# First loads moved from ScalarE's queue to SyncE's, planner durations reset, weight steps paced closer

## The chip, the cores and the metric

The kernel runs on one core of one Trainium2 chip. The metric is device microseconds of one execution, as the median of several runs. The engines are named as the profile names them: PE is TensorE (PEld its weight loads), DVE is VectorE, ACT is ScalarE, POOL is GpSimd, SP is SyncE. SPq and ACTq are the places where SP and ACT issue transfers.

## The reference

Clustered attention, followed by a softplus feed-forward layer. B, H, S, D = 4, 8, 768, 64, with 16 centroids for each head. A query sees only the keys that have the same nearest centroid.

```
q_assign = argmax(q_n @ c_n.T);  k_assign = argmax(k_n @ c_n.T)     # rows scaled to length 1
scores = where(q_assign == k_assign, (q @ k.T) / sqrt(D), -1e9)
attn = softmax(scores);  x = (attn @ v), heads put side by side     # 3072 x 512
h = x @ w_in                                                        # 512 x 2048
g = maximum(h, 0) + log1p(exp(-abs(h)))
out = g @ w_out                                                     # 2048 x 512
```

The two weights are float64 in memory; all else is float32.

## The kernel before

**Tiles.** The work is a list of 192 score tiles of 128 queries by 768 keys. A batch has two passes of three 128-row query blocks; each pass goes through 8 heads, so a pass is 24 tiles and tiles 0 to 23 are the first pass of the first batch. A tile is four score matmuls (`s`, L652), the row maximum on DVE (`negm`, L668) and the exponential on ACT (`p`, L676). The `negm` rows are a good clock: the n-th one is tile n.

**Two ways to go on.** In tiles 0 to 23 (`whole(t)`) the float32 probabilities are turned on PE (`pT`, L692), copied to SBUF by ACT or DVE (`ptf`, L248) and multiplied with raw values (L751, 12 records a tile). From tile 24 on they are split into two float16 halves by ACT (`phl`, L712) and POOL (L256). Two tiles together are transposed by one DMA on SP (`pt<-phl`, L275), and PE multiplies them with the values, 18 matmuls a tile (L755 to L757).

**Feed-forward.** When a pass has its 24 tiles, 16 steps of `h` follow (L833 to L835, 12 matmuls each), softplus on DVE and ACT, a split on ACT and POOL (`gh`), and the second product (L899 to L901) into `o`. They are spread between the tiles of later passes.

**Weights.** 32 steps turn float64 words into two float16 halves: a load of 512 KB by ACT (L270), an absolute value on ACT (L372), three integer operations on DVE (L374, L378, L384), a cast on ACT (L390) or DVE, and a subtraction on POOL (L256). Steps 0 to 15 make `wi`, 16 to 31 make `wo`. A step may not start ahead of tile `step * WPACE`.

**What sets the order.** Nothing runs as it comes: a planner (`Order`) simulates the five engines while the program is written. It takes each operation's assumed duration, given where the operation is yielded (`op("DVE", 680, ...)`), and a priority in tiles, and appends instructions to the engines' lists. The hardware then runs each list in order. So another number in the planner changes no instruction, but can change the order on every engine. `AHEAD` and `LAG` are the tiles by which feed-forward and the value products stand behind. Where the planner sees a gap over 600 ns on PE, `warm` fills part of it with matmuls whose result nobody reads (L227).

**Loads of the first batch** (`rawk`, `rawq`, `rawv`; 10 transfers of 384 KB) are issued by ACT like all loads. ACT also runs the two activations of the centroids' lengths (`cnrm`, L293 and L294).

Of the kernel before, what the change touches and what calls it, by code (L numbers as in the profile page):

```python
# [20 lines left out]
WGATE = 0  # L21
WPACE = 1.4
WDUE = 4
LAG = 4
AHEAD = 10
FIRST = 3
# [4 lines left out]
SLACK = 0  # L31
BIAS = 2000
WBIAS = 2000
# [7 lines left out]
class Order:  # L41
# [97 lines left out]
def tile_cluster_attention__then__softplus_ffn(  # L139
# [15 lines left out]
    P = 128  # L155
# [75 lines left out]
    def op(eng, ns, emit, **opt):  # L231
        return ("op", eng, ns, emit, opt)
# [10 lines left out]
    def evict(dst, src, size):  # L243

        return op(
            ("ACT", "DVE"),
            (180 + size * 0.8, 160 + size * 1.04),
            (lambda: nc.scalar.copy(dst, src), lambda: nc.vector.tensor_copy(dst, src)),  # L248
        )
# [18 lines left out]

    def load(dst, src, nbytes):
        return op("ACT", 60, lambda: nc.scalar.dma_start(dst, src), load=nbytes / 290.0)  # L270

# [9 lines left out]
    def prep_centroids():  # L281
# [4 lines left out]

        def dve(f, ns=100):
            return op("DVE", ns, f)

        yield op("DVE", 150, lambda: V.tensor_tensor(sq, cf, cf, ALU.mult))  # L290
        yield dve(lambda: V.tensor_reduce(ss, sq, AX.X, ALU.add))
# [25 lines left out]

        yield op("PE", 200, emit)
        yield op("ACT", 500, lambda: nc.scalar.copy(cents.rearrange("p a h c -> p a (h c)"), ps))
        od.set(hk)  # L320
# [15 lines left out]
    def prep_weights(step: int):  # L336
# [37 lines left out]
        yield op("DVE", 420, lambda: nc.vector.tensor_scalar(mab, mab, 3, None, ALU.logical_shift_left), shared=True)  # L374
        yield op(
            "DVE",
            680,
            lambda: nc.vector.scalar_tensor_tensor(high, high, -0x80000000, mab, ALU.bitwise_and, ALU.bitwise_or),  # L378
# [3 lines left out]
            "DVE",  # L382
            680,
            lambda: nc.vector.scalar_tensor_tensor(high, low, 29, high, ALU.logical_shift_right, ALU.bitwise_or),  # L384
# [35 lines left out]
    def prep_v(n: int):  # L420

        vk = yield from ring("vb", NP)
        rk, vf = yield from raw_tile("v", n, [P, 2, NT, D])
        yield load(vf, rows(v, n, 0, NT, 2), P * 2 * NT * D * 4)
        vb = VB[n // 2 % NP]
        raw_v[n] = vf, rk
        od.set(("vf", n))
        if n < H:
            od.cur["prio"] = H * QT
        yield op("ACT", 830, lambda: nc.scalar.copy(vb[:, :, :, D : 2 * D], vf))  # L430
        yield sub(vb[:, :, :, :D], vf, vb[:, :, :, D : 2 * D], NT * P)
# [7 lines left out]
    def turn(dst, src, name: str, on_chip: bool):  # L439

        if not on_chip:
            yield flip(dst, src.rearrange("p c d -> p (c d)"), dst.shape[1])
            return
        step = dst.shape[1] // 2
        for g in range(0, dst.shape[1], step):
            hk, ps = yield from bank(EARLY, [P, step, P], F16, f"{name}_{g}")

            def emit(g=g, ps=ps):
                for c in range(step):
                    nc.tensor.transpose(out=ps[:, c], in_=src[:, g + c], identity=eye)  # L450

            yield op("PE", 350, emit)
            yield evict(dst[:, g : g + step], ps, step * (P if dst.dtype == F32 else 100))
            od.set(hk)

    def nearest(sim, xs, heads, low: int, sfx: str):

        nt = len(xs)
        shp = [P, nt, NCL]
# [17 lines left out]
    def prep_k(n: int):  # L477

        kkey[n // 2] = yield from ring("kt", NP)
        rk, kf = yield from raw_tile("k", n, [P, 2, NT, D])  # L480
        yield load(kf, rows(k, n, 0, NT, 2), P * 2 * NT * D * 4)
        kf = kf.rearrange("p h c d -> p (h c) d")
# [37 lines left out]
    def clusters(n, ps, mask, hk):  # L520

        h = n % H
        cnt = ps[:, 2 * NT :]
        yield op("PE", 100, lambda: nc.tensor.matmul(cnt, ones, mask, start=True, stop=True))
        if h % 4 == 0:
            alive[n] = p2.tile([P, 4, NCL], F16, tag="al", name=f"al_{n}", bufs=4)
        al = alive[n - h % 4][:, h % 4 : h % 4 + 2]
        top = ps[:, :2]
        yield op(
            "DVE", 345, lambda: nc.vector.tensor_reduce(top, cnt.rearrange("p (u c) l -> p u l c", u=2), AX.X, ALU.max)  # L530
        )
        yield op("DVE", 190, lambda: nc.vector.tensor_scalar(al, top, -MASK * P, None, ALU.is_gt))
        od.set(hk)
        od.set(("al", n))

    def load_q(n: int, pi: int):

        _, c0, nt = passes[pi]
        rk, qf = yield from raw_tile("q", f"{n}_{pi}", [P, 4, nt, D])
        yield load(qf, rows(q, n, c0, nt, 4), P * 4 * nt * D * 4)  # L540
        return rk, qf
# [25 lines left out]
    def prep_q(n: int, pi: int, nh: int, qf, qt, rk):  # L567
        sfx = f"{n}_{pi}"
        nt = passes[pi][2]
        nx = nh * nt  # L570
        part = nx / 12
        qf = qf.rearrange("p h c d -> p (h c) d")
        k1 = yield from ring("n1", 2)
        n1 = p2.tile([P, nx, P], F16, tag="n1", name=f"qn1_{sfx}")
        yield op("ACT", 100 + 750 * part, lambda: nc.scalar.activation(n1[:, :, :D], qf, AF.Copy, scale=SCALE))
        yield op(
            "DVE",
            100 + 850 * part,
            lambda: nc.vector.scalar_tensor_tensor(n1[:, :, D:], qf, SCALE, n1[:, :, :D], ALU.mult, ALU.subtract),
# [12 lines left out]
        sim, best = yield from nearest(ps, [qt0[:, c] for c in range(nx)], heads, 1, f"q{sfx}")  # L592
        yield op("DVE", 345, lambda: nc.vector.tensor_tensor(sim, sim, best, ALU.is_equal))
        k2, n2 = yield from next_n2()
        n2 = n2[:, :nx]
        yield op("DVE", 345, lambda: nc.vector.tensor_scalar(n2[:, :, D : D + NCL], sim, MASK, None, ALU.mult))

        simh = sim.rearrange("p (u c) l -> p u c l", u=nh)
        if pi == 0:
# [9 lines left out]
        aq = p2.tile([P, nx, 1], F16, tag="aq", name=f"aq_{sfx}")  # L609
        yield op("DVE", 345, lambda: nc.vector.tensor_reduce(aq, sim, AX.X, ALU.max))  # L610
        od.set(hk)
        yield op(
            "POOL",
            100 + 1540 * part,
            lambda: nc.gpsimd.tensor_tensor(n2[:, :, :D], n1[:, :, :D], aq.to_broadcast([P, nx, D]), ALU.mult),
# [20 lines left out]
    def scores(t: int):  # L636
# [39 lines left out]
        yield op("ACT", 1095 if whole(t) else 900, lambda: nc.scalar.activation(p32, st[:, :, :SH], AF.Exp, bias=negm, **tot))  # L676
        od.set(sk)
        if whole(t):
# [8 lines left out]
            for j in range(2):  # L687
# [44 lines left out]
    def attend(t: int):  # L732
# [25 lines left out]

        yield op("PE", 1340 if whole(t) else 530, emit)
        od.set(("at", t))  # L760
# [15 lines left out]
        while c < 2 * nt:  # L776
            e = next((e for e in range(c, 2 * nt) if kinds[e] != kinds[c]), 2 * nt)
            weights = sums[n // 2][:, c:e] if kinds[c] else avt[:, c:e, D:]
            dst = rs[:, c:e]
            yield op("DVE", 150, lambda: nc.vector.tensor_scalar(dst, weights, 1e-9, None, ALU.add))  # L780
            c = e
# [213 lines left out]
```

## Time and profile before

| what | value |
|---|---|
| runs | 905.17 us median of 3 (903.13 to 906.0) |
| span of the profiled execution | 899.7 us, mean granted PE clock 0.994 |
| its own time beside the span | not listed; the median lies 5.5 us above the span |
| PE busy | 853.6 us, 95% |
| ACT, DVE, POOL busy | 66%, 61%, 59% |
| chain that ended last | 62% PE, 4% transposes `pt<-phl` |

A busy share is a mean over stages that have different limits. The stage rows below cut the span at tile 0, tile 24 and tile 72 and are read one by one. Windows of one line count the records that start there.

### The profile page before, as it was taken

To read this page: it belongs to the slowest core of one execution; us is meant where nothing else is said; L and a number is where in the kernel's file an instruction comes from. 1 tells how busy PE (TensorE), PEld (TensorE's weight loads), DVE (VectorE), ACT (ScalarE), POOL (GpSimd) and SP (SyncE) were. 2 spreads that over 40 slices of the span, in tenths; PEclk is the share of its full clock that TensorE was granted. 3 is DMA by queue.
4 is the path that set the end of the run, shared out by engine and by line. 5 is a ranking of instruction groups with operands and counts; after the bars stand their busy time and mean duration, and the time that the engine had idled before them with its cause. 6 is when DMAs were issued, how large, how long until landed. Compare 5 with 4: busy or idle time off the path is not lost.

```text
span 899.7 us, 21002 instructions
## 1 busy us (share of the span) xinstructions
PE 853.6 (95%) x8701; PEld 557.6 (62%) x8701; DVE 547.2 (61%) x1044; ACT 595.2 (66%) x920; POOL 528.9 (59%) x359
## 2 busy tenths in 40 slices
PE   6999977899888999999999999999999999999997
PEld 6788854666666556566666665666665665655554
DVE  5999885777767455575665565657665655433331
ACT  4887876777766757777667677787767676633330
POOL 5323576688766577677667577687666675512110
PEclk9999998999999999999999999999999999999999
DMA  6335499999986599999988999999977776610000
GB/s 223 120 118 119 110 219 199 193 178 218 220 180 138 126 202 182 185 215 204 178 149 163 153 176 187 205 202 192 175 151 153 121 127 137 123 31 15 22 1 36
DMA packets 392527, 135.94 MB, mean 151 GB/s; under 512 B 368880, under 2 KB 385264, under 8 KB 392432
## 3 DMA queue, kind: packets, MB, share of 16 engines
q1 hardware_dynamic: 370672, 98.95, 62.3%
q10 hardware_dynamic: 21760, 35.66, 13.2%
q8 instruction: 68, 1.11, 0.5%
q14 instruction: 27, 0.22, 0.1%
HBM read 35.68 MB, written 6.29 MB: 47 GB/s over the span
## 4 chain that ended last, share of the span: by engine, by line
PE 62%; DMA 4%; DVE 1%; issue 1%; POOL 1%; ACT 1%; POOLq 0%; ACTq 0%
PE s L652 8%; PE o L899 8%; PE o L901 8%; PE o L900 8%; PE h L833 7%; PE h L834 7%; PE h L835 7%; DMA pt<-phl 4%; PE mbank L755 3%; PE mbank L757 3%; PE mbank L756 2%; POOL phl L256 1%; DVE ot L919 0%; PE sim_q L464 0%; PE sim_q L463 0%
## 5 line engine op out<-in xcount | busy, mean ns | idle before, releaser
L256 POOL TENSOR_TENSOR phl<-p,phl 128x768 f16<-128x768 f32 x168 | 278.4, 1670 | 100.5 <-ACT phl L712 81.7
L668 DVE TENSOR_REDUCE negm<-s 128x1 f32<-128x768 f32 x192 | 182.9, 954 | 61.6 <-PE s L652 58.3
L676 ACT ACTIVATE p<-s,negm 128x768 f32<-128x768 f32 x192 | 172.5, 900 | 64.7 <-DVE negm L668 49.8
L256 POOL TENSOR_TENSOR gh<-fg,gh 128x768 f16<-128x768 f32 x64 | 107.1, 1675 | 144.7 <-ACT gh L876 144.6
L833 PE MATMUL h<-xT,wi 128*128 128x384 f16 x512 | 167.5, 327 | 5.5 <-DVE fg L865 5.5
L835 PE MATMUL h<-xT,wi 128*128 128x384 f16 x512 | 167.6, 327 | 0.0
L834 PE MATMUL h<-xT,wi 128*128 128x384 f16 x512 | 167.6, 327 | 0.0
L652 PE MATMUL s<-kt,qt 128*128 128x384 f16 x768 | 156.0, 325 | 3.4 <-ACT p L676 3.0
L712 ACT CAST phl<-p 128x768 f16<-128x768 f32 x168 | 136.4, 829 | 33.2 <-DMA pt<-phl 30.8
L901 PE MATMUL o<-wo,gh 128*128 128x512 f16 x384 | 145.5, 379 | 1.1 <-POOL gh L256 1.1
L899 PE MATMUL o<-wo,gh 128*128 128x512 f16 x384 | 145.5, 379 | 0.6 <-DVE ot L919 0.6
L900 PE MATMUL o<-wo,gh 128*128 128x512 f16 x384 | 145.5, 379 | 0.0
L855 ACT ACTIVATE fa<-fa 128x384 f32<-128x384 f32 x128 | 66.6, 520 | 109.9 <-DVE fa L853 109.5
L853 DVE TENSOR_SCALAR fa<-h 128x384 int32<-128x384 int32 x128 | 71.1, 556 | 110.1 <-PE h L835 109.8
L755 PE MATMUL mbank<-vb,pt 128*128 128x65 f16 x1008 | 109.1, 193 | 17.5 <-DMA pt<-phl 17.5
L755 PEld LDWEIGHTS <-pt 128*128 128x128 f16 x1008 | 93.8, 98 | 32.4 <-DMA pt<-phl 21.7
L756 PE MATMUL mbank<-vb,pt 128*128 128x64 f16 x1008 | 109.0, 193 | 0.0
L757 PE MATMUL mbank<-vb,pt 128*128 128x65 f16 x1008 | 108.7, 195 | 0.0
L865 DVE SCALAR_TENSOR_TENSOR fg<-h,fa 128x384 f32<-128x384 f32 x128 | 70.6, 552 | 59.2 <-ACT fa L856 54.4
L652 PEld LDWEIGHTS <-qt 128*128 128x128 f16 x768 | 71.7, 98 | 48.0 <-issue 4.8
L756 PEld LDWEIGHTS <-pt 128*128 128x128 f16 x1008 | 93.4, 97 | 10.6 <-issue 0.2
L757 PEld LDWEIGHTS <-pt 128*128 128x128 f16 x1008 | 93.5, 97 | 0.0
(121 smaller groups left out, 1277.1 us busy)
## 6 DMA issues: line engine op xcount, KB each, us to landing
wo<-in_moe_w_in_dram ACTq DMA_DIRECT2D x16, 512.0 KB, 3.6
wo<-in_moe_w_out_dram ACTq DMA_DIRECT2D x14, 512.0 KB, 5.9
rawk<-in_k_dram ACTq DMA_DIRECT2D x16, 384.0 KB, 5.0
rawq<-in_q_dram ACTq DMA_DIRECT2D x16, 384.0 KB, 5.0
rawv<-in_v_dram ACTq DMA_DIRECT2D x16, 384.0 KB, 5.7
out_dram<-ot SPq DMA_DIRECT2D x24, 256.0 KB, 2.6
pt<-phl SPq DMA_TRANSPOSE x84, 6.7
wraw<-in_moe_w_out_dram ACTq DMA_DIRECT2D x2, 512.0 KB, 4.9
```

Of the source, the lines that this page charges most:

```text
L256: [lambda e=e: e.tensor_tensor(dst, a, b, ALU.subtract) for e in (nc.gpsimd, nc.vector)],
L652: nc.tensor.matmul(st[:, j, :SH], qt[:, s, i], kt[:, s, NT // 2 * j : NT // 2 * (j + 1)], start=(s == 0), stop=(s == 1),)
L668: yield op("DVE", 950, lambda: nc.vector.tensor_reduce(negm, st[:, :, :SH], AX.XY, ALU.max, negate=True))
L755: nc.tensor.matmul(av, pt[:, 0, c], vb[:, c, D : 2 * D + 1], start=(c == 0), stop=False)
L756: nc.tensor.matmul(av[:, :D], pt[:, 0, c], vb[:, c, :D], start=False, stop=False)
L757: nc.tensor.matmul(av, pt[:, 1, c], vb[:, c, D : 2 * D + 1], start=False, stop=(c == NT - 1))
L833: nc.tensor.matmul(hp, w[0], x[0], start=(c == 0), stop=False)
L834: nc.tensor.matmul(hp, w[0], x[1], start=False, stop=False)
L835: nc.tensor.matmul(hp, w[1], x[0], start=False, stop=(c == NP - 1))
L899: nc.tensor.matmul(po, g[0], wo[:, f, 0, 0], start=(f == f0), stop=False)
L900: nc.tensor.matmul(po, g[0], wo[:, f, 0, 1], start=False, stop=False)
L901: nc.tensor.matmul(po, g[1], wo[:, f, 0, 0], start=False, stop=(f == f0 + NF // 2 - 1))
```

## The change

The loads of batch 0 (`n < H`, or pass 0 for queries) are issued by SP; all others stay on ACT. Most assumed durations get other values, the engines no longer start at time 0 in the planner, and five constants change. No instruction's kind or size changes.

```
-WPACE = 1.4
-WDUE = 4
-LAG = 4
-AHEAD = 10
+WPACE = 0.8
+WDUE = 2
+LAG = 6
+AHEAD = 8
...
-BIAS = 2000
+BIAS = 1000
...
-        self.free = dict.fromkeys(self.LAT, 0.0)
+        self.free = {"PE": 1800.0, "DVE": 2500.0, "ACT": 2000.0, "POOL": 4800.0, "SP": 1000.0}
...
-            (180 + size * 0.8, 160 + size * 1.04),
+            (155 + size * 0.855, 155 + size * (1.04 if wide else 0.52)),
...
-    def load(dst, src, nbytes):
-        return op("ACT", 60, lambda: nc.scalar.dma_start(dst, src), load=nbytes / 290.0)
+    def load(dst, src, nbytes, first=False):
+
+        if first:
+            return op("SP", 500, lambda: nc.sync.dma_start(dst, src), load=nbytes / 340.0)
+        return op("ACT", 350, lambda: nc.scalar.dma_start(dst, src), load=nbytes / 340.0)
...
-        yield load(vf, rows(v, n, 0, NT, 2), P * 2 * NT * D * 4)
+        yield load(vf, rows(v, n, 0, NT, 2), P * 2 * NT * D * 4, n < H)
...
-            680,
+            760,
             lambda: nc.vector.scalar_tensor_tensor(high, high, -0x80000000, mab, ALU.bitwise_and, ALU.bitwise_or),
```

Line numbers shift by 4 to 6: L248 is then L249, L374 L378, L378 L382, L384 L388, L668 L674.

**ACT at the start of the program.** `rawk`, `rawq`, `rawv` are the first batch's loads, `kn` the first use of a load. Before:

```order
L270 DMA rawk_130<-in_k_dram 128x2x384
L270 DMA rawq_0_131<-in_q_dram 128x4x192
L270 DMA wo<-in_moe_w_in_dram 128x512
L270 DMA rawv_132<-in_v_dram 128x2x384
L293 ACTIVATE cnrm<-csg 128x1
L270 DMA rawk_133<-in_k_dram 128x2x384
L294 ACTIVATE cnrm<-cnrm 128x1
L270 DMA rawv_134<-in_v_dram 128x2x384
L319 COPY cents<-centsT 128x384
L496 CAST kn_0_137<-rawk_125 128x12x64
L575 ACTIVATE qn_0_0_142<-rawq_0_126 128x6x64
```

Now:

```order
L167 ACT_TABLE_LOAD
L274 DMA wo<-in_moe_w_in_dram 128x512
L297 ACTIVATE cnrm<-csg 128x1
L298 ACTIVATE cnrm<-cnrm 128x1
L501 CAST kn_0_136<-rawk_125 128x12x64
L581 ACTIVATE qn_0_0_141<-rawq_0_126 128x6x64
L581 ACTIVATE qn_2_0_142<-rawq_0_126 128x6x64
L434 CAST vb_104<-rawv_127 128x12x64
```

Ten issues left ACT's list and stand on SP behind the centroids' load, one weight load stands ahead of `cnrm`, and the first cast no longer stands behind the copy of the centroids (`cents`).

**DVE at tiles 12 to 15**, in the first pass. `wi` and `wo` rows belong to weight steps, `ptf` and `qt` rows are copies out of PSUM. Before:

```order
L668 TENSOR_REDUCE negm_0_1217<-s_0_1180 128x1
L384 SCALAR_TENSOR_TENSOR wo<-wo 128x512
L374 TENSOR_SCALAR wi<-wi 128x512
L248 COPY ptf_1_1169<-pT_2_0_1220 128x384
L668 TENSOR_REDUCE negm_1_1245<-s_1_1219 128x1
L579 SCALAR_TENSOR_TENSOR qn_0_1_1192<-rawq_1_1181,qn_0_1_1192 128x12x64
L248 COPY ptf_0_1235<-pT_0_0_1236 128x384
L248 COPY ptf_0_1235<-pT_1_0_1264 128x384
L378 SCALAR_TENSOR_TENSOR wo<-wo,wi 128x512
L668 TENSOR_REDUCE negm_2_1274<-s_2_1244 128x1
```

Now:

```order
L674 TENSOR_REDUCE negm_0_1245<-s_0_1189 128x1
L249 COPY qt_0_158<-qT_6_0_0_1296 128x384
L382 SCALAR_TENSOR_TENSOR wo<-wo,wi 128x512
L378 TENSOR_SCALAR wi<-wi 128x512
L249 COPY qt_0_158<-qT_6_0_3_1319 128x384
L388 SCALAR_TENSOR_TENSOR wo<-wo 128x512
L382 SCALAR_TENSOR_TENSOR wo<-wo,wi 128x512
L249 COPY ptf_1_1313<-pT_1_1_1342 128x384
L674 TENSOR_REDUCE negm_1_1340<-s_1_1316 128x1
L388 SCALAR_TENSOR_TENSOR wo<-wo 128x512
L378 TENSOR_SCALAR wi<-wi 128x512 x2
L382 SCALAR_TENSOR_TENSOR wo<-wo,wi 128x512
```

Between two neighbouring row maxima there now stand more weight rows.

**SP where tiles 46 to 49 are transposed**, at the start of the second batch. `pt` rows are the transposes of two tiles, `kt` and `qt` those of keys and queries, `xT` those of attention's result. Before:

```order
L275 DMA_TRANSPOSE pt_5_3317<-phl_4_3165 128x24x128
L275 DMA_TRANSPOSE kt_2764<-n_1_114 128x12x128
L275 DMA_TRANSPOSE pt_1_3414<-phl_0_3207 128x24x128
L275 DMA_TRANSPOSE kt_3227<-kn_14_3226 128x12x128
L275 DMA_TRANSPOSE pt_0_3512<-phl_2_3333 128x24x128
```

Now:

```order
L279 DMA_TRANSPOSE pt_5_3322<-phl_4_3066 128x24x128
L279 DMA_TRANSPOSE qt_2_2825<-n_0_112 128x12x128
L279 DMA_TRANSPOSE kt_3257<-kn_12_3256 128x12x128
L279 DMA_TRANSPOSE xT_2528<-xn_1_3532 128x6x128
L279 DMA_TRANSPOSE kt_3451<-kn_14_3450 128x12x128
L279 DMA_TRANSPOSE kt_3257<-n_1_114 128x12x128
L279 DMA_TRANSPOSE pt_1_3654<-phl_0_3573 128x24x128
```

Between the pair of tiles 46 and 47 and the pair 48 and 49 there stood one other transpose; now there stand five.

More of the change, by code (lines that the diff above doesn't have):

```diff
@@ L285, in prep_centroids, with dve @@
         V = nc.vector
-        def dve(f, ns=100):
+        def dve(f, ns=195):
             return op("DVE", ns, f)
-        yield op("DVE", 150, lambda: V.tensor_tensor(sq, cf, cf, ALU.mult))
+        yield op("DVE", 1050, lambda: V.tensor_tensor(sq, cf, cf, ALU.mult))
         yield dve(lambda: V.tensor_reduce(ss, sq, AX.X, ALU.add))
@@ L316, in emit @@
                 nc.tensor.transpose(out=ps[:, a], in_=cb[:, a].rearrange("p j d -> p (j d)"), identity=eye)
-        yield op("PE", 200, emit)
-        yield op("ACT", 500, lambda: nc.scalar.copy(cents.rearrange("p a h c -> p a (h c)"), ps))
+        yield op("PE", 580, emit)
+        yield op("ACT", 480, lambda: nc.scalar.copy(cents.rearrange("p a h c -> p a (h c)"), ps))
         od.set(hk)
@@ L452, in turn @@
             yield op("PE", 350, emit)
-            yield evict(dst[:, g : g + step], ps, step * (P if dst.dtype == F32 else 100))
+            yield evict(dst[:, g : g + step], ps, step * P)
             od.set(hk)
@@ L458, in nearest @@
         nt = len(xs)
+        ns = 145 + 17.5 * nt
         shp = [P, nt, NCL]
@@ L480, in prep_k @@
         rk, kf = yield from raw_tile("k", n, [P, 2, NT, D])
-        yield load(kf, rows(k, n, 0, NT, 2), P * 2 * NT * D * 4)
+        yield load(kf, rows(k, n, 0, NT, 2), P * 2 * NT * D * 4, n < H)
         kf = kf.rearrange("p h c d -> p (h c) d")
@@ L523, in clusters @@
         cnt = ps[:, 2 * NT :]
-        yield op("PE", 100, lambda: nc.tensor.matmul(cnt, ones, mask, start=True, stop=True))
-        if h % 4 == 0:
-            alive[n] = p2.tile([P, 4, NCL], F16, tag="al", name=f"al_{n}", bufs=4)
+        yield op("PE", 180, lambda: nc.tensor.matmul(cnt, ones, mask, start=True, stop=True))
+        if n - h % 4 not in alive:
+            alive[n - h % 4] = p2.tile([P, 4, NCL], F16, tag="al", name=f"al_{n - h % 4}", bufs=4)
         al = alive[n - h % 4][:, h % 4 : h % 4 + 2]
@@ L529, in clusters @@
         yield op(
-            "DVE", 345, lambda: nc.vector.tensor_reduce(top, cnt.rearrange("p (u c) l -> p u l c", u=2), AX.X, ALU.max)
+            "DVE", 360, lambda: nc.vector.tensor_reduce(top, cnt.rearrange("p (u c) l -> p u l c", u=2), AX.X, ALU.max)
         )
@@ L539, in load_q @@
         rk, qf = yield from raw_tile("q", f"{n}_{pi}", [P, 4, nt, D])
-        yield load(qf, rows(q, n, c0, nt, 4), P * 4 * nt * D * 4)
+        yield load(qf, rows(q, n, c0, nt, 4), P * 4 * nt * D * 4, pi == 0)
         return rk, qf
@@ L609, in prep_q @@
         aq = p2.tile([P, nx, 1], F16, tag="aq", name=f"aq_{sfx}")
-        yield op("DVE", 345, lambda: nc.vector.tensor_reduce(aq, sim, AX.X, ALU.max))
+        yield op("DVE", ns, lambda: nc.vector.tensor_reduce(aq, sim, AX.X, ALU.max))
         od.set(hk)
@@ L675, in scores @@
             tot["accum_out"] = sums[n // 2][:, n % 2 * nt + i]
-        yield op("ACT", 1095 if whole(t) else 900, lambda: nc.scalar.activation(p32, st[:, :, :SH], AF.Exp, bias=negm, **tot))
+        yield op("ACT", 1105 if whole(t) else 895, lambda: nc.scalar.activation(p32, st[:, :, :SH], AF.Exp, bias=negm, **tot))
         od.set(sk)
@@ L757, in emit @@
                 nc.tensor.matmul(av, pt[:, 1, c], vb[:, c, D : 2 * D + 1], start=False, stop=(c == NT - 1))
-        yield op("PE", 1340 if whole(t) else 530, emit)
+        yield op("PE", 1310 if whole(t) else 530, emit)
         od.set(("at", t))
@@ L779, in attend @@
             dst = rs[:, c:e]
-            yield op("DVE", 150, lambda: nc.vector.tensor_scalar(dst, weights, 1e-9, None, ALU.add))
+            yield op("DVE", 220, lambda: nc.vector.tensor_scalar(dst, weights, 1e-9, None, ALU.add))
             c = e
```

34 lines of the change are left out of this document (18 added, 16 removed).

## Prediction

> **What bounds the kernel now.** I read the page's shares, then the busy time by stage, then PE's waits in the stage that loses most, then the rows at the stage's ends. The stages are cut at the row maxima of tiles 0, 24 and 72, and at 860 us.
>
> ```profile
> 29.20 0.95 DVE L668 TENSOR_REDUCE negm<-s 128x1 f32<-128x768 f32 x1
> 103.03 0.94 DVE L668 TENSOR_REDUCE negm<-s 128x1 f32<-128x768 f32 x1
> 312.35 0.96 DVE L668 TENSOR_REDUCE negm<-s 128x1 f32<-128x768 f32 x1 [0.99 <-PE s L652]
> ...
> 0.00:29.20 29.20, 20.70 (x328) 19.10 (x329) 17.81 (x83) 16.68 (x26) 18.13 (x23) 0.94 0.60 199
> 29.20:103.00 73.80, 70.73 (x717) 62.66 (x715) 68.39 (x136) 59.71 (x122) 21.34 (x20) 1.00 0.43 115
> 103.00:312.35 209.35, 182.70 (x2198) 128.63 (x2197) 147.61 (x258) 150.54 (x229) 145.80 (x98) 0.98 0.91 182
> 312.35:860.00 547.65, 545.21 (x5235) 328.56 (x5234) 305.13 (x556) 360.59 (x533) 338.75 (x218) 1.00 0.81 151
> 860.00:899.70 39.70, 34.23 (x233) 18.70 (x231) 8.29 (x14) 7.65 (x13) 4.92 (x3) 1.00 0.06 21
> ```
>
> Columns: stretch, its length, busy PE, PEld, DVE, ACT, POOL, granted clock, DMA share, GB/s. PE is idle for 8.5 us in the head, 3.1 in the first pass, 26.7 in the middle, 2.4 from tile 72 to 860 us and 5.5 in the tail. Behind tile 72 the kernel is PE and nothing else. In the first pass DVE is busy for 68.4 of 73.8 us, as much a bound as PE. In the middle the DMA engines are busy for 91%, PE for 87%.
>
> Part of PE's busy time is filler:
>
> ```profile
> 29.20:103.00 73.80, 6.33 (x96) 5.50 (x93) 1.00 0.43 115
> 103.00:312.35 209.35, 32.19 (x523) 29.42 (x523) 0.98 0.91 182
> 312.35:860.00 547.65, 0.00 (x0) 0.00 (x0) 1.00 0.81 151
> 877.29 3.52 PE L227 MATMUL mbank<-ones,eye 128*128 128x120 f16 x64
> ```
>
> These are the rows of L227 alone. A filler takes 3.52/64 = 0.055 us, so the middle's 523 take 28.8. With the 26.7 idle, PE has nothing useful to do for 55 of 209 us there. What it waits for, where the planner put no filler:
>
> ```profile
> PE mbank L755 <- DMA pt<-phl: 15.0, 7, 5.7
> PE h L833 <- DVE fg L865: 5.5, 8, 1.6
> ...
> 142.18 10.06 SPq L275 DMA_TRANSPOSE pt<-phl  x1
> 150.90 0.24 PE L755 MATMUL mbank<-vb,pt 128*128 128x65 f16 x1 [5.69 <-DMA pt<-phl]
> ```
>
> The middle is bound by transposes that share the DMA engines with loads. One took 10 us to issue, and PE stood still for 5.7 us.
>
> PE's list has the same useful matmuls before and after, and 843 fillers for 852, which is 0.5 us. So the change is worth what PE's idle time changes by, and less than 46 us.
>
> **Loads from SP, and ACT's new order at the start.** Now the first cast stands at 10.83 us:
>
> ```profile
> 0.74 0.39 SPq L186 DMA_DIRECT2D cf<-in_centroids_dram  x1
> 0.77 0.45 ACTq L270 DMA_DIRECT2D rawk<-in_k_dram  x1
> 3.85 0.15 DVE L292 TENSOR_SCALAR csg<-css 128x1 f32<-128x1 f32 x1
> 4.41 1.28 ACTq L270 DMA_DIRECT2D wo<-in_moe_w_in_dram  x1
> 6.50 0.20 ACT L293 ACTIVATE cnrm<-csg 128x1 f32<-128x1 f32 x1 [4.49 <-issue]
> 7.47 0.38 ACTq L270 DMA_DIRECT2D rawv<-in_v_dram  x1
> 10.46 0.48 ACT L319 COPY cents<-centsT 128x384 f16<-128x384 f16 x1 [3.17 <-PE centsT L316]
> 10.83 0.84 ACT L496 CAST kn<-rawk 128x768 f16<-128x768 f32 x1
> ...
> DMA to landing us min/median/max: 3.6/6.7/8.6
> ```
>
> The last row is that of `rawk` in the first 40 us. Its earliest landing is 3.6 us behind the issue, at 4.4, while the cast waits for the copy of the centroids in its queue. That hangs on `cnrm`, which waited 4.49 us behind issues. Now the cast stands behind `cnrm` alone: `csg` is there at 4.00, two activations and the gap between them take it to about 4.9, and `rawk`, issued by SP at 1.13, lands at 4.7. That is 5.9 us earlier. SP's ten issues at about 0.5 us end near 6.1, and the last load lands by 6.1 + 8.6 = 14.7, no later than now (7.47 + 8.6). Nothing is queued on SP behind them until the first transpose of the first pass, so SP pays nothing. The ends are 0 (tile 0 waits for something unmoved) and -5.9. DVE gets four more copies ahead of tile 0, and the centroids' copy now stands behind more casts, so I take **-4**.
>
> The Trainium skill (DMA: Bandwidth & Descriptors, "Issuing engines are not separate DMA queues") says that transfers from all issuing engines interleave on the same 16 DMA engines, and that a second issuing engine saves only issue time. By that the data come no earlier, and if landing were the limit this term would be 0 and the sum 4 us less good. Here the earliest landing, 4.4 us, is far ahead of its use at 10.83, so issue time and queue order are what counts.
>
> **Weight steps closer, `WPACE` and `WDUE`.** Up to tile 24 DVE's order held 15, 15 and 13 rows of L374, L378 and L384; now it holds 20 of each. Their busy time in the first pass, in this order:
>
> ```profile
> 29.20:103.00 73.80, 6.38 (x15) 1.00 0.43 115
> 29.20:103.00 73.80, 11.18 (x15) 1.00 0.43 115
> 29.20:103.00 73.80, 9.80 (x13) 1.00 0.43 115
> ```
>
> Five by 0.43, five by 0.75 and seven by 0.75 us make 11.1 us more DVE work in the first pass. Copies out of PSUM stay about even (21 and 22). ACT gains seven casts and four absolute values and loses six copies, and has 14 us idle; POOL gains seven subtractions and has 52 idle. DVE has only 5.4 us idle. If all of it were used, the pass grows by 5.7; if the busy share stays at 93%, by 12.0. Waits between engines seldom vanish when an engine gets fuller; still, some idle time should be used: **+9.5**.
>
> PE gets 167 more fillers there (order rows from tile 0 to 24: 267 for 100), 9.2 us, so the loss will look like filler.
>
> **Fewer loads in the middle.** Six of sixteen weight loads leave it for the first pass, where the DMA engines are busy for only 43%. Their price:
>
> ```profile
> q1 hardware_dynamic: 95223, 24.26, 68.3%
> q10 hardware_dynamic: 7073, 13.48, 22.4%
> ...
> wo<-in_moe_w_out_dram ACTq DMA_DIRECT2D x14, 512.0 KB, 5.9
> ```
>
> These are the middle's queues. q10, the loads, takes 22.4% of 209.35 = 46.9 us for 13.48 MB, 3.5 us per MB, so 1.82 us for 512 KB; six are 10.9 us. If the DMA engines set the stage's length, it is -10.9; if the chain of score, maximum, exponential, split and transpose does, it is 0. At 91% busy, with 15.0 us of PE waiting for `pt`, I take **-10.9**. Seven weight steps less on DVE and POOL come off engines that are 70% busy and cost nothing.
>
> **`AHEAD`, `LAG` and the durations.** Ahead of tile 72 PE's order had 360 matmuls of L833 to L835 and 108 of L899 to L901; now 330 and 168. Value products are equal. Their spacing:
>
> ```profile
> 243.08 0.33 PE L833 MATMUL h<-xT,wi 128*128 128x384 f16 x1
> 243.24 0.33 PE L834 MATMUL h<-xT,wi 128*128 128x384 f16 x1
> ...
> 872.97 0.38 PE L900 MATMUL o<-wo,gh 128*128 128x512 f16 x1
> 873.19 0.38 PE L901 MATMUL o<-wo,gh 128*128 128x512 f16 x1
> ```
>
> Thirty by 0.16 less and sixty by 0.22 more are 8.4 us of work done earlier, out of a stretch that is all PE. It is worth -8.4 if it fills waits in the middle, and 0 if it pushes tile 72 back by as much. The 55 us without useful work leave room, but its inputs need not be ready in time: **-4.5**. The tail's order is the same, at nothing.
>
> **The sum**: -4 + 9.5 - 10.9 - 4.5 - 0.5 = -10.4, so a span near 889 us, and 5.5 above it a median of **895**.
>
> One more thing lies inside the range. After the stall at 150.90, PE is slow:
>
> ```profile
> 152.17 0.53 PE L834 MATMUL h<-xT,wi 128*128 128x384 f16 x1
> 152.49 0.53 PE L835 MATMUL h<-xT,wi 128*128 128x384 f16 x1
> ...
> 156.04 0.53 PE L834 MATMUL h<-xT,wi 128*128 128x384 f16 x1
> ```
>
> Spacing is 0.32 for 0.16 us for at least 5.1 us, so the spell cost about 2.6 us beside the wait. If this stall goes, it comes off too; a new one of this length would add it.
>
> The Trainium skill (TensorE: Matmul & The Clock Gate, "What's actually happening") says that an idle window of about 3.4 us halves PE's clock, and a busy one of that length restores it. By that figure the spell costs 1.7 us. The trace has it longer, and its number stands.
>
> **Rivals.**
> - *DVE in the first pass decides; the middle gives nothing back* (slower). For it: 68.4 of 73.8 us; and 5.5 us of PE's waits in the middle are for softplus on DVE, which no load delays. Against it: the 10 us issue and the `pt` waits. Time: -2 + 12.0 + 0 + 0 - 0.5 = +9.5, 914.7. It decides once tile 24 is late by more than the middle returns: at +6 or more against less than 6.
> - *They cancel.* SP's order has five other transposes between the pairs of tiles 46/47 and 48/49, where one stood. Each moves 6 or 12 blocks, a quarter or half of a pair's 24, so four more stop the flow of tiles for about one and a half pairs. If PE's feed-forward backlog doesn't cover that, the relief of 10.9 is lost there: -10.4 + 10.9 = +0.5, 905.7.
> - *The middle's waits go as well.* If the durations now fit the chip, PE finds its inputs in time. Then the 15.0 for `pt` and the 2.6 of the slow spell go too, instead of the 10.9: -4 + 9.5 - 17.6 - 8.4 - 0.5 = -21, 884. Against it: transposes still fill 68% of the middle.
> - *The change does nothing.* The orders differ on every engine, so it isn't a separate case; it is within the second.
>
> **Chances.** 0.3% is 2.7 us, about what a measurement of this kernel tells from no change. My sum (between -3 and -15): 0.40. The larger gain: 0.22. Cancelled: 0.14. Slower: 0.24. So faster 0.62, same 0.14, slower 0.24. From the bounds, the sum's own range goes from -5.9 + 5.7 - 10.9 - 8.4 - 0.5 = -20 to 0 + 12.0 - 10.9 - 0 - 0.5 = +0.6. The range reaches into both neighbours, leaving a tenth on each side: 881 to 912. The likeliest case's own is 885 to 906.
>
> **What would show it.** Tile 0's `negm` near 25 us and the first cast near 5. Tile 24 near 108.5 with DVE over 93% busy and more filler. Tile 72 at 307 to 311, 10 weight loads between it and tile 24, under 10 us of PE waiting for `pt`, no spell of 0.32 spacing in the middle. I am wrong if tile 24 is as early as tile 0's gain says (the DVE term), if tile 72 comes behind 312 with the DMA share well under 0.9 (the DMA term), or if PE is idle for more than 5 us behind tile 72.

## The result, and the profile after

The changed kernel took 899.54 us, the median of 20 runs (894.53 to 909.69), against 904.76 for the kernel before in the same series (20 runs, 896.84 to 909.92). The ratio is 0.9941 with a 95% interval of 0.992 to 0.9963: faster by about 0.6%, where the prediction forecast 895.0 in a range from 881 to 912. Here and below, a ratio leaves out the executions that were more than 1.5% above the fastest of their kernel, while medians and ranges count all, so a ratio is not quite the quotient of two medians. The profiled execution after lasts 899.86 us and its span is 897.6, so 2.2 us lie outside the span.

The stages after, cut at the row maxima of tiles 0, 24 and 72 (27.3, 110.6 and 320.7 us) and at 860 us; columns as in the prediction's stage rows:

```profile
27.29 0.95 DVE L674 TENSOR_REDUCE negm<-s 128x1 f32<-128x768 f32 x1
...
320.66 0.96 DVE L674 TENSOR_REDUCE negm<-s 128x1 f32<-128x768 f32 x1 [0.26 <-PE s L658]
```

```profile
0.00:27.30 27.30, 21.76 (x321) 19.73 (x322) 19.27 (x85) 15.43 (x25) 18.45 (x23) 0.94 0.69 233
27.30:110.60 83.30, 77.69 (x869) 69.02 (x869) 77.88 (x157) 62.96 (x127) 29.31 (x26) 1.00 0.48 128
110.60:320.70 210.10, 186.72 (x2072) 127.45 (x2072) 143.34 (x242) 140.65 (x212) 138.39 (x92) 0.96 0.91 172
320.70:860.00 539.30, 538.71 (x5214) 326.58 (x5213) 309.96 (x560) 362.98 (x539) 334.94 (x218) 1.00 0.81 152
860.00:897.60 37.60, 32.52 (x224) 17.75 (x222) 7.20 (x13) 6.67 (x11) 4.92 (x3) 1.00 0.06 22
```

The head is 1.9 us shorter, the first pass 9.5 longer, the middle 0.75 longer, and everything behind tile 72 takes 576.9 us for 587.35, 10.4 less. PE's filler (rows of the filler line alone, by the same columns for PE and PEld) moved from the middle to the first pass:

```profile
27.30:110.60 83.30, 16.62 (x267) 15.31 (x267) 1.00 0.48 128
110.60:320.70 210.10, 22.92 (x348) 21.62 (x348) 0.96 0.91 172
```

In the middle, PE's longest waits (total us, times, longest) and the queues and weight loads:

```profile
PE mbank L761 <- DMA pt<-phl: 10.3, 3, 5.0
PE s L658 <- ACT p L682: 5.6, 7, 2.5
...
PE h L839 <- DVE fg L871: 2.8, 5, 0.7
```

```profile
q1 hardware_dynamic: 99055, 25.68, 72.6%
q10 hardware_dynamic: 5462, 10.17, 17.8%
...
wo<-in_moe_w_out_dram ACTq DMA_DIRECT2D x8, 512.0 KB, 5.2
...
wraw<-in_moe_w_out_dram ACTq DMA_DIRECT2D x2, 512.0 KB, 6.1
```

The ten weight loads that were forecast are there (8 and 2). The waits for `pt` fell from 15.0 to 10.3 us and from seven to three, but those left are long ones.

**The books.** PE's time splits into useful work, waiting, filler (0.055 us each), and time lost to the granted clock (one minus the clock, times the length, summed over windows of 2.5 us; called half clock, since the clock is at half in these spells). Half clock while PE is idle counts in both rows. In us, before and after:

| | head | first pass | middle | behind tile 72 | sum |
|---|---|---|---|---|---|
| PE idle | 8.5, 5.5 | 3.1, 5.6 | 26.7, 23.4 | 7.9, 5.7 | 46.1, 40.2 |
| filler | 8.3, 7.8 | 5.3, 14.7 | 28.8, 19.1 | 4.7, 4.7 | 47.1, 46.4 |
| half clock | 1.7, 1.7 | 0, 0 | 3.4, 8.5 | 0, 0 | 5.1, 10.2 |

What is left is 801.3 and 800.8 us: the same useful work. So the 2.1 us between the two spans are 5.9 less idle, 0.7 less filler, 5.1 more half clock, and 0.5 in the remainder. In the middle, idle and filler fell by 13.0 us, half clock took 5.1 back, and the 8.4 us of feed-forward that now run ahead of tile 72 used what was left; that is why the middle is as long as before and the stretch behind it shorter.

The two profiled executions stand only 2.1 us apart while the medians stand 5.2 apart. In the runs since, 1.8 us lie outside the span of the kernel before, so its profile (899.7) was of an execution near 901.5, one of its shorter ones. Its clock was high as well: 0.994 in the profile, and 0.990 as the mean of the 87 executions of this kernel that ran beside the experiments, on three chips; only 13 of them reach 0.994. After, the profile has 0.989 and the mean of the 20 executions is 0.987. One minus the mean clock, times the span, is 9.3 us of half clock before and 11.7 after. By this estimate usual executions stand about 2.4 us apart in half clock, where the two profiled ones stand 5.1 apart.

### The profile page after: what moved, and what is told of

The parts are those of the page before. It is cut to its first block, busy times and chain, and to the rows that moved or that the text cites. A ratio compares the mean times of both kernels' runs of the same rounds, so it can differ in the third digit from the quotient of the medians.

```text
span 897.6 us, 20963 instructions
## 1 busy us (share of the span) xinstructions
PE 857.4 (96%) x8692; PEld 560.5 (62%) x8692; DVE 557.6 (62%) x1051; ACT 588.7 (66%) x913; POOL 526.0 (59%) x359
## 4 chain that ended last, share of the span: by engine, by line
PE 70%; DVE 6%; DMA 6%; POOL 2%; issue 2%; ACT 2%; POOLq 0%; DVEq 0%; ACTq 0%
PE s L658 10%; PE o L907 9%; PE o L905 8%; PE o L906 8%; PE h L839 8%; PE h L840 8%; PE h L841 8%; DMA pt<-phl 6%; PE mbank L761 3%; PE mbank L763 3%; PE mbank L762 3%; DVE negm L674 1%; POOL phl L257 1%; DVE wo L382 1%; PE mbank L227 1%
## 5 line engine op out<-in xcount | busy, mean ns | idle before, releaser
L674 DVE TENSOR_REDUCE negm<-s 128x1 f32<-128x768 f32 x192 | 182.6, 953 | 52.0 <-PE s L658 47.1
L718 ACT CAST phl<-p 128x768 f16<-128x768 f32 x168 | 136.4, 828 | 28.8 <-DMA pt<-phl 27.3
L761 PE MATMUL mbank<-vb,pt 128*128 128x65 f16 x1008 | 110.6, 194 | 10.6 <-DMA pt<-phl 10.3
L762 PE MATMUL mbank<-vb,pt 128*128 128x64 f16 x1008 | 110.6, 193 | 0.0
L763 PE MATMUL mbank<-vb,pt 128*128 128x65 f16 x1008 | 110.3, 195 | 0.0
```

The source lines that it names most:

```text
L674: yield op("DVE", 950, lambda: nc.vector.tensor_reduce(negm, st[:, :, :SH], AX.XY, ALU.max, negate=True))
L761: nc.tensor.matmul(av, pt[:, 0, c], vb[:, c, D : 2 * D + 1], start=(c == 0), stop=False)
L762: nc.tensor.matmul(av[:, :D], pt[:, 0, c], vb[:, c, :D], start=False, stop=False)
L763: nc.tensor.matmul(av, pt[:, 1, c], vb[:, c, D : 2 * D + 1], start=False, stop=(c == NT - 1))
```

## Experiments

All ratios are to the kernel before on the same chip, with 95% intervals. No ratio to the kernel after was measured; where two ratios are set against each other, they come from different chips, and each has its interval.

**The loads alone, without a new plan.** The kernel before, with the ten first loads issued by SP. The planner still counts them as ACT's 60 ns, so its order doesn't change.

```
+        if first:
+            return op("ACT", 60, lambda: nc.sync.dma_start(dst, src), load=nbytes / 290.0)
...
-        yield load(vf, rows(v, n, 0, NT, 2), P * 2 * NT * D * 4)
+        yield load(vf, rows(v, n, 0, NT, 2), P * 2 * NT * D * 4, n < H)
```

> The kernel before with every list in its old order, but the ten first loads issued by SP. Only the queue moves, the plan does not. If the free ACT queue is worth something by itself, tile 0 comes 1 to 3 us earlier than 29.2 and the ratio is 0.996 to 0.999. Rival: the head is bound by the casts and subtractions that follow, or the middle swallows the gain: 0.999 to 1.002. What the kernel with the loads alone replanned (0.989) gains beyond this is then the planner's other order.

898.34 us (12 runs), 0.9961 [0.9922, 0.9999]. Row maxima of tiles 0, 47, 48, 60 and 72, of this kernel and then of the kernel before:

```profile
26.32 0.94 DVE L670 TENSOR_REDUCE negm<-s 128x1 f32<-128x768 f32 x1
...
194.61 0.95 DVE L670 TENSOR_REDUCE negm<-s 128x1 f32<-128x768 f32 x1
197.28 0.96 DVE L670 TENSOR_REDUCE negm<-s 128x1 f32<-128x768 f32 x1
...
263.12 1.81 DVE L670 TENSOR_REDUCE negm<-s 128x1 f32<-128x768 f32 x2
...
311.51 0.96 DVE L670 TENSOR_REDUCE negm<-s 128x1 f32<-128x768 f32 x1 [0.99 <-PE s L654]
```

```profile
201.41 0.95 DVE L668 TENSOR_REDUCE negm<-s 128x1 f32<-128x768 f32 x1
204.08 0.96 DVE L668 TENSOR_REDUCE negm<-s 128x1 f32<-128x768 f32 x1
...
264.25 0.94 DVE L668 TENSOR_REDUCE negm<-s 128x1 f32<-128x768 f32 x1
```

Tile 0 is 2.9 us earlier (26.32 against 29.20) and tile 48 still 6.8 (197.28 against 204.08); by tile 60 only 1.1 are left, by tile 72 0.8. A gain at the head is carried to the second batch, and most of it is given back there. At ACT's start in this kernel:

```profile
7.60 0.48 ACT L321 COPY cents<-centsT 128x384 f16<-128x384 f16 x1 [3.16 <-PE centsT L318]
7.98 0.83 ACT L498 CAST kn<-rawk 128x768 f16<-128x768 f32 x1
```

The copy of the centroids moved from 10.46 to 7.60, by as much as tile 0.

**The loads back on ACT, in the new plan.** The kernel after; the planner still counts them as SP's 500 ns.

```
-            return op("SP", 500, lambda: nc.sync.dma_start(dst, src), load=nbytes / 340.0)
+            return op("SP", 500, lambda: nc.scalar.dma_start(dst, src), load=nbytes / 340.0)
```

> The changed kernel with every list in the same order, but the ten first loads issued by ACT again, at the place where the planner put them. If the head's gain comes from ACT's queue freed of issues (about 0.5 us each, ten of them), tile 0 comes 2 to 5 us later than the 27.3 us of the changed kernel and the ratio to the kernel before rises from 0.994 to 0.996 to 0.999. Rival: the gain at the head is given back in the first pass, which DVE bounds, or the move of the loads was never what counted; then the ratio stays at 0.993 to 0.995.

899.84 us (12 runs), 0.9989 [0.9954, 1.0024]. The median is that of the kernel after; the ratio is 0.5% higher, and the two intervals overlap from 0.9954 to 0.9963. What the edit costs is not settled: nothing by the medians, 0.5% by the ratios. The trace:

```profile
30.26 0.95 DVE L674 TENSOR_REDUCE negm<-s 128x1 f32<-128x768 f32 x1
...
230.55 0.94 DVE L674 TENSOR_REDUCE negm<-s 128x1 f32<-128x768 f32 x1
...
284.68 0.96 DVE L674 TENSOR_REDUCE negm<-s 128x1 f32<-128x768 f32 x1 [0.99 <-PE s L658]
```

```profile
227.70 0.96 DVE L674 TENSOR_REDUCE negm<-s 128x1 f32<-128x768 f32 x1
...
284.29 0.96 DVE L674 TENSOR_REDUCE negm<-s 128x1 f32<-128x768 f32 x1 [0.99 <-PE s L658]
```

Above are tiles 0, 48 and 60 of this kernel, below tiles 48 and 60 of the kernel after. The 3.0 us at tile 0 are there as 2.9 at tile 48 and 0.4 at tile 60. Both traces give the same reading: the head's 3 us reach the second batch and are mostly lost between tiles 48 and 60.

**The loads with a new plan.** The kernel before with the loads planned and issued on SP, `op("SP", 500, ...)`, and nothing else.

> The kernel before with the first ten loads on SP alone (planned with 500 ns each on SP). If the head's 2 to 4 us reach the end, tile 0 is at 25 to 27.5 us and the ratio 0.995 to 0.998. Rival: the middle swallows them, or the planner's other order decides: 0.998 to 1.005.

896.53 us (6 runs), 0.9887 [0.9844, 0.9929]. It is the lowest ratio of a kernel that does all the work; its interval overlaps that of the kernel after, so it is shown to beat the kernel before and not the kernel after. The head has nothing to do with it: in its profiled execution tile 0 stands at 35.7 us, 6.5 later than before, and tile 72 at 327.8. That execution is the longest of the six. Its books are 40.8 idle, 48.5 filler, 8.6 half clock. Ratio and tile 0 lie outside both expected ranges.

**The pace alone, in the old plan and out of the new one.** Before with `WPACE` 0.8 and `WDUE` 2; after with 1.4 and 4.

> The kernel before with WPACE 0.8 and WDUE 2 alone. If pulling the weight steps forward is what shortens the kernel (loads leave the middle, which the DMA engines bound), the ratio is 0.988 to 0.994, with tile 24 5 to 9 us later than 103.0. Rival: what the middle gains, the longer first pass takes: 0.997 to 1.003.

906.22 us (12 runs), 1.0006 [0.9974, 1.0038]; tile 0 at 29.4 us, tile 24 at 112.0, tile 72 at 324.9. The first pass takes 82.6 us for 73.8, of which 3.4 are half clock. Alone, the pace takes only two weight loads out of the middle (14 issues between tiles 24 and 72 for 16), not six as the whole change does.

> The changed kernel with WPACE 1.4 and WDUE 4 again, planned anew: 102 fillers more (5.6 us), six or seven weight loads back in the middle. If loads in the middle cost their full DMA price, as the light loads showed (12.5 us for 12.7), tile 24 comes near 101, but tile 72 no earlier than 320, and the ratio is 0.998 to 1.006. Rival: the shorter first pass makes up for it, as in the kernel before with the new pace alone (1.0006): 0.992 to 0.997.

903.18 us (12 runs), 0.9995 [0.9968, 1.0022]; tile 0 at 27.2 us, tile 24 at 104.4, tile 72 at 322.9. The first pass takes 77.3 us for 83.3, and 16 weight loads are back in the middle. So the pace is worth nothing in the old plan, and about 0.5% in the new one (0.9995 against 0.9941, whose intervals just fail to overlap). In both plans it makes the first pass longer, by 8.8 and by 6.0 us; what comes back for that hangs on the rest of the plan.

**The durations alone.** Before with the new durations, start times and `BIAS`, the loads still on ACT (350 ns).

> The kernel before with the new assumed durations, start times and BIAS alone (loads on ACT, old pace, LAG and AHEAD). If durations that fit the chip remove waits by themselves, PE's idle time falls under 35 us from 46 and the ratio is 0.985 to 0.995. Rival: the planner's order is as good or bad as before, and 79 more fillers cost up to 4 us: 0.998 to 1.008.

914.77 us (6 runs), 1.0102 [1.0065, 1.0139]. Tile 0 stands at 39.1 us. The new durations alone made the kernel slower by 1%, more than either expected range. The parts alone (loads 0.9887 or 0.9961, pace 1.0006, durations 1.0102) do not add up to the whole: each makes its own order on every engine and its own number of fillers (882, 834 and 931, where the whole change has 843).

**`LAG` and `AHEAD` back.** After with 4 and 10.

> The changed kernel with LAG 4 and AHEAD 10 again, planned anew. If feed-forward moved ahead is what the change gains (8.4 us of work ahead of tile 72), the ratio goes back to 0.999 to 1.005. Rival: these two only push work about, and idle, filler and cold time stay within 3 us of the changed kernel's 97 us: 0.991 to 0.997.

899.61 us (12 runs), 0.9947 [0.9917, 0.9976]: no different from the kernel after. It does not test what the feed-forward ahead of tile 72 is worth: in its trace 320 matmuls of `h` and 162 of `o` stand there, 332 and 168 in the kernel after, so the new plan took back only 3.2 of the 8.4 us.

**Lighter weight loads in the middle.** After; the eight `wo` loads of the middle bring 64 of 512 columns, and most of those weights are left out.

```
+        cols = WC // 8 if step >= 22 and room < 8 else WC
+        yield load(raw64[:, :cols], src[:, c, e * WC : e * WC + cols], P * WC * 8)
```

> The changed kernel in the same order, but eight weight loads of steps 22 to 29 bring only 64 of 512 columns, so that 8 x 7/8 x 1.82 = 12.7 us of load work leave the DMA engines in the middle stage (tiles 24 to 71). It leaves out most of those weights. If the share of busy DMA engines sets the middle's length, the middle shrinks from 210 us to 197 to 201 and the ratio falls to 0.980 to 0.985. Rival: the middle is set by the chain of score, maximum, exponential, split and transpose and by where the planner put the work of the second batch, and loads only stretch what nobody waits for; then the middle shrinks by less than 4 us and the ratio is 0.989 to 0.995.

887.52 us (6 runs), 0.982 [0.9781, 0.9859]. Seven eighths of eight loads at 1.82 us are 12.7 us of transfer; the span is 12.7 us shorter than that of the kernel after, and tile 72 comes 12.5 earlier:

```profile
308.16 0.96 DVE L675 TENSOR_REDUCE negm<-s 128x1 f32<-128x768 f32 x1 [0.26 <-PE s L659]
```

By the ratios it is 1.2%, about 11 us. So in an order that is kept, a load taken out of the middle is worth its full time. The books show how: idle falls from 40.2 to 32.8 us and half clock from 10.2 to 5.1. One place in both traces, first the kernel after (a weight load on ACT's queue, three transposes on SP with the time in which the first of them landed, PE's next product with values, PE's next steps of `h`), then this kernel (the same first transpose, its landing, the transpose of keys, the product):

```profile
171.44 0.38 ACTq L274 DMA_DIRECT2D wo<-in_moe_w_out_dram  x1
```

```profile
169.82 3.87 SPq L279 DMA_TRANSPOSE pt<-phl  x1
...
175.44 7.41 SPq L279 DMA_TRANSPOSE kt<-kn  x1
183.01 4.91 SPq L279 DMA_TRANSPOSE pt<-phl  x1
...
DMA to landing us min/median/max: 13.2/13.2/13.2
```

```profile
183.03 0.23 PE L761 MATMUL mbank<-vb,pt 128*128 128x65 f16 x1 [4.98 <-DMA pt<-phl]
...
184.31 0.53 PE L840 MATMUL h<-xT,wi 128*128 128x384 f16 x1
184.62 0.53 PE L841 MATMUL h<-xT,wi 128*128 128x384 f16 x1
```

```profile
170.87 3.51 SPq L279 DMA_TRANSPOSE pt<-phl  x1
...
DMA to landing us min/median/max: 9.1/9.1/9.1
...
176.17 3.59 SPq L279 DMA_TRANSPOSE kt<-kn  x1
...
180.03 0.20 PE L762 MATMUL mbank<-vb,pt 128*128 128x65 f16 x1 [0.92 <-DMA pt<-phl]
```

PE waits here for the transpose issued at 169.82, not for one behind it. With the full loads it lands 13.2 us behind its issue, PE waits 4.98 us for it, and then works at a spacing of 0.31 for 0.16. With the light ones it lands after 9.1 us, PE waits 0.92 and keeps its clock. The transpose of keys, issued while it was on its way, takes 7.41 us to issue in the one and 3.59 in the other.

**Lighter integer operations in the first pass.** After; the three integer operations of weight steps 0 to 19 on 64 of 512 columns, which leaves most of the conversion out.

```
+        part_ = WC // 8 if step < 20 else WC
...
+        yield op("DVE", 450, lambda: nc.vector.tensor_scalar(mab[:, :part_], mab[:, :part_], 3, None, ALU.logical_shift_left), shared=True)
```

> The changed kernel in the same order, but the three integer operations on DVE of weight steps 0 to 19 work on 64 of 512 columns, which takes some 30 us of DVE work out of the first pass. It leaves out most of that conversion. If DVE sets the first pass, tile 24 comes earlier than 110.6 us until PE with its fillers is the limit (5.6 us idle there): 105 to 107, and the ratio falls to 0.987 to 0.990 if the rest keeps it. Rival: the first pass is set by PE's list with its 14.7 us of filler; then tile 24 moves by less than 2 us and the ratio stays at 0.992 to 0.995.

895.34 us (12 runs), 0.9904 [0.9872, 0.9936]. The first pass of its profiled execution, in the stage columns:

```profile
28.40:109.10 80.70, 76.88 (x864) 68.55 (x864) 55.37 (x156) 61.98 (x126) 27.34 (x26) 1.00 0.47 129
```

DVE's busy time falls from 77.88 to 55.37 us, and the pass shortens by 2.6. With DVE at 69% the pass is nearly as long as with DVE at 93%, so in this order DVE's work alone does not set its length. More than 5.6 us could not come back, though: the filler stays in PE's list, and with it PE is busy for 77.7 of the 83.3 us in the kernel after. Whether the planner would put the filler there with less DVE work is not tested.

**No filler in the first pass.** After, with none of the fillers between tiles 0 and 24.

```
+        first_pass = ("sc", 0) in od.ev and ("sc", 23) not in od.ev
+        if gap > WARM_FROM and not first_pass:
```

> The changed kernel in the same order, without the 257 fillers that stand between tile 0 and tile 24 (14.1 us at 0.055). If PE's list with its fillers sets the first pass, it shrinks from 83.3 us to 70 to 76 and the ratio to the kernel before falls to 0.982 to 0.990, if the middle keeps it. Rival: the fillers only cover waits for DVE and ACT; then the first pass shrinks by less than 3 us, PE is idle instead, and the ratio stays at 0.992 to 0.998, or is worse if PE goes to half clock there.

908.59 us (12 runs), 1.0027 [0.999, 1.0064]. Its profiled execution, 916.39 us, is the longest of the twelve, so its lengths are above the usual ones; its first pass:

```profile
28.40:123.30 94.90, 80.46 (x612) 68.32 (x612) 76.61 (x157) 62.93 (x127) 29.53 (x26) 0.82 0.38 112
```

In this execution the granted clock falls from 1.00 to 0.82 and the pass grows from 83.3 to 94.9 us. The fall is not its own alone: the mean clock of all twelve is 0.974, for 0.987 after. So leaving the filler out gains nothing, since the clock falls without it; how long the pass would be without filler at a full clock this run does not show.

**More filler.** After with `WARM_SHARE` 0.9 for 0.65 (1176 fillers for 843).

> The changed kernel in the same order, but with 1176 fillers instead of 843, in the same places: 333 by 0.055 are 18 us more filler. If they fall into time in which PE would be idle or cold, the spells at half clock get fewer and the time stays within 3 us or falls: ratio 0.989 to 0.997. Rival: the gaps that the planner sees are already filled or are not there on the chip, and each filler delays useful work: 8 to 18 us longer, ratio 1.003 to 1.014.

897.11 us (12 runs, 894.5 to 898.63), 0.9911 [0.9884, 0.9938]. Stages 29.7 to 115.5 to 316.6 us:

```profile
29.70:115.50 85.80, 81.90 (x973) 74.31 (x972) 77.53 (x156) 63.24 (x127) 28.89 (x26) 1.00 0.45 124
115.50:316.60 201.10, 187.87 (x2212) 130.97 (x2211) 139.96 (x242) 140.93 (x212) 139.56 (x92) 0.99 0.97 181
```

The first pass is 2.5 us longer and the middle 9.0 shorter, at a clock of 0.99 for 0.96. Its books: 27.2 idle, 64.7 filler, 5.4 half clock, together 97.2 where the kernel after has 96.8. Over its twelve executions the mean clock is 0.9925, so half clock is less in usual executions too. The 3.0 us between the two spans lie in the remainder (797.4 for 800.8), which the books don't explain. The ratios differ by 0.3% and their intervals overlap: no gain is shown, but the executions lie closer together.

**More filler in the loads' own plan.** `WARM_SHARE` 0.9 in the kernel that has the loads planned on SP (1230 fillers for 882).

> The kernel before with the first ten loads planned and issued on SP, and with 1230 fillers for 882 in the same places. If filler ends spells at half clock and takes only idle time, as it did for the changed kernel (0.991 for 0.994), idle and cold time fall by more than the 19 us that the filler costs, and the ratio is 0.982 to 0.988. Rival: this order has fewer cold spells to end (8.6 us in its profile), so the filler costs what it brings: 0.988 to 0.993.

903.66 us (12 runs), 1.001 [0.9976, 1.0043], above both expected ranges. The mean granted clock of its profiled execution is 0.998 against 0.991 without the added filler. Idle falls by 14.0 us to 26.8 and half clock by 6.9 to 1.7, but filler rises by 19.2 to 67.7, so nearly all is taken back. The profiled pair flatters the added filler (spans 896.1 and 899.4, the latter its kernel's longest execution): the mean clock is 0.994 over the twelve executions with it and 0.9945 over the six without, so usual executions lose no less to half clock. Then 19.2 us of filler stand against 14.0 of idle, an estimate of 5.2 us longer, where the medians stand 7.1 apart (903.66 and 896.53).

## Why the prediction came near, step by step

**The total.** 895.0 was forecast and 899.54 measured, inside the range and on the forecast side. The sum forecast -10.4 us; the medians show half of it, -5.2, and the profiled pair -2.1. The 5.5 us that the prediction laid between span and median are not time outside the span, which is 1.8 to 2.2 us; the rest is that the execution profiled before was a short one. With 2 us its span near 889 would have meant 891; the 5.5 made the forecast the median before less 10.4, so this misreading did the total good. The range also holds the times of two rivals (884 and 905.7), so the time alone does not bear out the mechanism; the terms do that, one by one.

**The head, -4: measured -1.9.** The first cast moved as worked out:

```profile
4.17 0.20 ACT L297 ACTIVATE cnrm<-csg 128x1 f32<-128x1 f32 x1 [2.16 <-DVE csg L296]
...
5.69 0.83 ACT L501 CAST kn<-rawk 128x768 f16<-128x768 f32 x1 [1.08 <-DMA rawk<-in_k_dram]
...
11.75 0.48 ACT L323 COPY cents<-centsT 128x384 f16<-128x384 f16 x1 [0.37 <-PE centsT L320]
```

It is 5.1 us earlier, at 5.69 and now waiting for `rawk`'s landing, but the new plan put the copy of the centroids 1.3 us later. With the old order this copy and tile 0 both moved by 2.9 us. The prediction saw that copy stand behind more casts and priced it too low, it seems; no run puts the copy back by itself. The Trainium skill (DMA: Bandwidth & Descriptors, "Issuing engines are not separate DMA queues") grants another issuing engine only issue time. The trace agrees: tile 0's 2.9 us in the old order are issue time, less than the ten issues of about half a microsecond that left ACT's list.

**The first pass, +9.5: measured +9.5, for a reason that is only partly right.** The pass grew by what was forecast and its filler by 9.4 us. But with 22.5 us taken off DVE it gave back only 2.6, of the 5.6 that the filler in PE's list left to be had. And the pace alone made the pass 8.8 us longer in the old plan with only 2.1 us more DVE work in it (70.5 for 68.4), DVE at 85% and 3.4 us at half clock. So added DVE work need not be what lengthens it, and the prediction's step from DVE's work to the pass's length is not borne out. The pace causes it, as both pace runs show; by which part (ACT's casts, the planner's order around the weight steps, the filler it then adds) is open.

**The middle, -10.9, and the feed-forward ahead, -4.5: measured +0.75 and -10.4 together.** This is the step that was off: -15.4 with the prediction's own reading, -9.7 in the traces. What it priced did come. The lighter loads bear out the price of a load (12.5 to 12.7 us for 12.7). Idle and filler fell by 13.0 us in the middle and idle by 2.2 behind tile 72, and the 8.4 us of feed-forward left that stretch. What the sum lacked is the half clock: the middle lost 8.5 us to it, after 3.4 before. The prediction named such a spell, put 2.6 us on one, and left it in the range. Between usual executions the half clock of the whole span differs by 2.4 us and not by 5.1, as worked out above. With the 2.1 us that the head fell short, that is 4.5 of the 5.2 us by which the medians miss the sum; this is an estimate, since one execution of each kernel was profiled. The prediction's reading of the stall before was off in one point: the transpose that took 10.06 us to issue released nobody who waited. PE's 5.69 us were for the one issued before it, at 134.12, which landed 16.7 us later.

In the trace after, the half clock is a term of its own:

```profile
150.00:175.00 25.00, 24.29 (x318) 17.18 (x318) 19.53 (x32) 21.11 (x33) 21.87 (x15) 1.00 1.04 196
175.00:200.00 25.00, 18.10 (x198) 12.39 (x197) 15.46 (x25) 14.70 (x23) 11.89 (x9) 0.84 0.97 163
200.00:225.00 25.00, 23.31 (x254) 15.08 (x253) 11.04 (x26) 10.89 (x18) 16.58 (x12) 0.96 1.06 195
225.00:250.00 25.00, 19.30 (x205) 12.67 (x203) 20.02 (x37) 14.66 (x22) 11.09 (x8) 1.00 0.86 160
250.00:275.00 25.00, 22.04 (x242) 15.24 (x243) 13.31 (x27) 15.01 (x23) 13.36 (x10) 0.93 0.59 127
```

From 175 to 200 us PE is idle for 6.9 us and loses 4.0 more (16% of 25) to the clock, with the DMA engines at 97%.

**The rival "they cancel".** Its place is in the trace: between tile 47 (193.32 us) and tile 48 (227.70) no tile comes for 34.4 us, where before the longest gap there was 13.6, between tiles 46 and 47. The five transposes stand there, and tiles 44 to 48 take 53.9 us for 22.7. But tiles 24 to 44 had come in 63.2 us for 78.4, and PE is busy for 23.3 of the 25 us from 200 to 225. The kernel with lighter loads has a gap of the same kind (31.4 us), and its tile 72 comes 12.5 us earlier, so the gap alone does not eat the relief. What the gap itself costs no run shows.

**The other rivals.** "DVE decides" is out by its own condition: tile 24 came 7.6 us late, more than its 6, but the middle and the stretch behind it gave back 9.7, and the kernel is faster. "The middle's waits go as well" came true in part: 4.7 of the 15.0 us of waits for `pt` went, and the half-clock spells grew.

**Its signs.** The first cast (5.69 us), tile 24 (110.6 for 108.5) and the ten loads came as said. Tile 0 came at 27.3 for 25, tile 72 at 320.7 for 307 to 311, PE waited 10.3 us for `pt` for under 10, and spells of half clock stayed. Of its sign against the load term, tile 72 behind 312 with the DMA share well under 0.9, only the first half is met: the share is 0.91.

**What stays open.** Why the plan with the loads alone does as well as or better than the whole change, when its tile 0 is 6.5 us later and all 16 weight loads are still in its middle. Part of it is the clock: the mean of its six executions is 0.9945, 4.9 us of half clock, for 9.3 before and 11.7 after. What in that order keeps the clock up no run here separates.

## What to carry to other kernels

When a planner fixes the order, price the edit's own part on its own, by changing only what is emitted and leaving the planner's numbers alone; a part that is replanned tells of a new order, not of the part. Keep books of PE's idle, filler and half-clock time by stage, since their sum is what an order can change: the useful remainder stayed between 797 and 802 us in all fourteen kernels profiled here. Before a term is read from two profiles, set their granted clocks beside the means of all executions; here half of the difference in half clock lay in which executions were profiled. Where transfers and transposes shared the DMA engines at 91%, the loads taken away in a kept order were worth their full transfer time, part of it (5.1 of 12.7 us) through the clock.

## What the runs showed of the hardware

- A stall of PE costs more than itself. After the 4.98 us wait the clock is granted at half, in windows of 2.5 us:

```profile
182.50:185.00 2.50, 1.97 (x22) 1.46 (x23) 0.00 (x0) 1.99 (x3) 1.03 (x1) 0.50 1.25 234
185.00:187.50 2.50, 2.50 (x24) 1.70 (x23) 1.35 (x2) 2.26 (x4) 2.22 (x2) 0.50 0.99 273
187.50:190.00 2.50, 2.50 (x14) 1.37 (x13) 1.29 (x3) 2.20 (x4) 1.47 (x2) 0.80 1.30 256
```

  The clock falls about 3.6 us into the wait, at 181.7 us, and is back at full at about 188.5, 5.5 behind the end of the wait: a spell of 6.8 us. In the fourteen traces each of the 51 spells that end inside the span lasts 3.41 us or a whole multiple of it, so the losses in the books are multiples of 1.7 us. The Trainium skill (TensorE: Matmul & The Clock Gate, "What's actually happening") has the clock halve after an idle window of about 3.4 us and come back after a busy one, with windows that run freely of the kernel. The trace agrees in the length. But a shorter wait can do it too: the spell from 123.65 us in the kernel after begins in a wait of 2.50 us, with PE busy for 1.53 of the 3.3 us ahead of it, while the wait of 0.92 us left the clock at full.
- The spread between executions goes with the clock: over 87 runs of the kernel before, a mean granted clock higher by 0.01 goes with about 7 us less (correlation -0.61).
- Filler matmuls pay where they stand against such spells (without them the first pass fell to a clock of 0.82, and the mean of twelve executions to 0.974) and cost their own time where more of them do not raise the clock (1.001, with a mean of 0.994 for 0.9945).
- A load lengthens the transposes beside it. In the place shown, with eight 512 KB loads cut to 64 KB, a transpose of two tiles landed after 9.1 us for 13.2, and the issue of the next transpose of keys on SP took 3.59 us for 7.41.
